# Mixing with features folded a second time, rows exchanged through DRAM, and the first chunk's norm moved

## The chip, the cores and the metric

One core of a Trainium2 chip runs the whole kernel. The metric is the device time of an execution in microseconds. Engines: PE is TensorE (matmuls; PEld its weight loads), DVE VectorE, ACT ScalarE, POOL GpSimd, SP the engine that issues the DMAs.

## The reference

Attention with a sigmoid in place of the softmax, for 8 batches, 12 heads, 448 tokens, 64 features a head; then a mixing layer by Fourier transforms over tokens and features, and a feed-forward net:

```
scores = q @ k.T / sqrt(64) - log(448);  attn = sigmoid(scores);  x = (attn @ v)   as [8, 448, 768]
u  = x + real(fft(fft(x, axis=1), axis=2))
un = (u - mean(u)) / sqrt(var(u) + 1e-6)          over the 768 features
y  = u + relu(un @ w_ch1) @ w_ch2                 768 -> 3072 -> 768
```

All inputs and outputs are float32.

## The kernel before

**Stages.** The 3584 rows (8 batches of 448) go through attention and mixing batch by batch, and `u` is stored to DRAM (`u_dram`). Then the feed-forward net runs on seven chunks of 512 rows: the first plainly (`up_proj`, `down_proj`), interleaved with the end of the mixing, the other six with a fast matrix product of seven partial products (`fast_up`, `fast_down`). In the attention stage the weights are also read, split and stored again (`weight`, 48 blocks), and brought into their final form (`pair`) from step 180 on.

**The steps of the attention stage.** The loop `for t in range(0, TQ + 12, 2)` is an order written out by hand. A batch has 24 steps, a group of four heads eight. In each pass PE gets scores, the functions that `at(t, ...)` has put into `extra` for two steps are called in the order in which they were put there, then the values (`values`) or, in every fourth pass, a part of the mixing (`mix_some`) follow. `pin` ties the instructions of each engine to this order, so every engine works strictly in it.

**The folds.** `values` leaves x transposed in `xT` [128 features, 6 blocks, 2 halves of tokens, 225]. Blocks p and p + 3 make a pair. `fold` makes six additions or subtractions a pair, 18 a batch, all on POOL: features d and d + 384 (level 0, `eo`), the two halves of the tokens (level 1, `fd`), tokens n and 224 − n (level 2, into `xp`). `FOLDS` names their steps: pair 0 at 12 to 17, pair 1 at 20 to 25, pair 2 at 28 and 29, when its block is there.

**The mixing.** From step 34 of a batch on its pieces stand in the list `units`, and the first part is run at step 36, the others at 44 and 52. `stage_d` transforms along the features: for each `kp`, `c` (cosine or sine) and parity `par` of the frequency, three matmuls with 193 columns of `cd_sb` add up the three pairs. ACT copies the result to `A`. `stage_s` transforms along the tokens with 385 columns; ACT copies one result to `Q`, DVE forms `sm` and `df`. `add_x` transposes x on PE, three blocks at a time, and DVE adds it: `u`. SP stores the rows. The last batch's mixing runs after the loop, between pieces of `up_proj`.

**The norm of the first chunk** (`norm`, two groups of 256 rows): load (n = 0), statistics (1), the reciprocal root in small DVE instructions on [128, 2] (`rsqrt`, 2 to 5), scaling on DVE (7), a float16 copy `hl` on ACT (8), the rest on DVE and two transposing DMAs on SP for each 128 rows (9). `hl` has one buffer. `norm_plan` gives the steps, `at(96 + 32 * g + n, fn)` their start.

**ACT's other work** in the stage: `sigmoid` after every score product, `cast`, the absolute value of the weights, `xT`. All DMAs are issued by SP.

Of the kernel before, what the change touches and what calls it, by code (L numbers as in the profile page):

```python
# [19 lines left out]
HM = 113  # L20
HS = 225
# [4 lines left out]
CP = 128  # L26
CH = 64
# [4 lines left out]
FOLDS = ((12, 13, 14, 15, 16, 17), (20, 21, 22, 23, 24, 25), (28, 28, 28, 29, 29, 29))  # L32
# [19 lines left out]
def spectral_attention_ffn(tc, qk, v, w1, w2, cd, cs, ident_in, out):  # L52
# [8 lines left out]
    with ExitStack() as top:  # L61
# [4 lines left out]
        w_dram = dram.tile([2, NP, 128, 2, 7, 384], F16, name="w_dram")  # L66
        ident = cpool.tile([128, 128], F32, name="ident")
# [13 lines left out]
        if True:  # L81
# [87 lines left out]
            def values(gg, w):  # L169
                b, r = divmod(gg, NG)  # L170
                p = r + 3 * w
                vr, ps = vrs[gg], avs[gg][w]
                for c in range(3):
                    a = att.pop((2 * gg + w, c))
                    for j in range(2):
                        h = c * 256 + (2 * w + j) * D
                        nc.tensor.matmul(  # L177
                            ps[j * D:(j + 1) * D, :SQ], vr[:, h:h + D], a[:, j], start=False, stop=(c == 2))
                if r == 0 and w == 0:
                    xp = wst[0].tile([128, 2, 8, 384], F16, tag="ws", name="xp", bufs=3)  # L180
                    xp = xp.rearrange("p x s n -> p (x s n)").bitcast(F32)[:, :24 * HM]
                    xts[b] = (fx.tile([128, 6, 2, HS], F32, tag="xT", name="xT", bufs=2),
                              xp.rearrange("p (f c r i s) -> p f c r i s", f=2, c=2, r=2, i=3))
# [3 lines left out]
            eos = {}  # L187

            def fold(b, p, n, e):

                xT, xp = xts[b]
                lv, n = divmod(n, 2)
                op = (ALU.add, ALU.subtract)[n]
                if lv == 0:
                    if n == 0:
                        eos[p] = [fx.tile([128, 2, 2, HS], F32, tag=t, name=t) for t in ("eo", "fd")]
                    e.tensor_tensor(out=eos[p][0][:, n], in0=xT[:, p], in1=xT[:, p + 3], op=op)  # L197
                elif lv == 1:
                    eo, fd = eos[p]
                    e.tensor_tensor(out=fd[:, n], in0=eo[:, :, 0], in1=eo[:, :, 1], op=op)  # L200
                else:
                    fd = eos[p][1]
                    e.tensor_tensor(
                        out=xp[:, n, :, :, p], in0=fd[:, :, :, 0:HM], in1=fd[:, :, :, HS - 1:HM - 2:-1], op=op)

            def mix_units(b):
                xT, xp = xts[b]
                A = fx.tile([HM, 2, 2, 386], F32, tag="A", name="A")
                ps_d, sd, ut = {}, {}, {}

                def stage_d(kp, c, par, p):
                    m = HM - kp
                    if par == 0 and p == 0:
                        ps_d[c, kp] = ps_m.tile([128, 512], F32, tag="m", name="psd")
                    ps = ps_d[c, kp]
                    nc.tensor.matmul(
                        ps[:HM, par * 193:par * 193 + 193], xp[:, kp ^ c, c, par, p],
                        cd_sb[:, c, par, p], start=(p == 0), stop=(p == 2))
                    if par == 1 and p == 2:
                        act_next.append(lambda: nc.scalar.activation(  # L220
                            A[:, kp, c].rearrange("s (i r) -> s r i", r=2),
                            ps[:HM, 0:386].rearrange("s (r i) -> s r i", r=2), AF.Copy))

                def stage_s(kp, c):
# [3 lines left out]
                        ps[:m, :385], cs_sb[:HM, kp, c, :m], A[:, kp, c, :385], start=True, stop=True)  # L228
                    if c == 1:
                        sd["Q", kp] = Q = fx.tile([128, 385], F32, tag="Q", name="Q", bufs=2)  # L230
                        act_next.append(lambda: nc.scalar.activation(Q[:m], ps[:m, :385], AF.Copy))
                    else:
                        Q = sd["Q", kp]
                        sd[kp] = [fx.tile([128, 385], F32, tag=n, name=n) for n in ("sm", "df")]
                        for o, op in zip(sd[kp], (ALU.add, ALU.subtract)):
                            dve_next.append(lambda o=o, op=op: nc.vector.tensor_tensor(
                                out=o[:m], in0=ps[:m, :385], in1=Q[:m], op=op))

                def add_x(kp, r, hf):
# [7 lines left out]
                    for i in range(3):  # L247
                        nc.tensor.transpose(
                            ps[:HM - kp, i * 128:(i + 1) * 128], xT[:, hf * 3 + i, r, kp:HS:2], ident)
                    y = d if hf == r else s  # L250
                    m = HM - kp
                    ysl = y[:m, 384:0:-1] if hf else y[:m, 0:384]

                    def add():
                        nc.vector.tensor_tensor(
                            out=u[:m, hf * 384:hf * 384 + 384], in0=ps[:m, :384], in1=ysl, op=ALU.add)
# [11 lines left out]
                def units_d(kp, c):  # L268
                    return [(0.33, lambda par=par, p=p: stage_d(kp, c, par, p)) for par in range(2) for p in range(3)]
# [59 lines left out]
            def weight_row():  # L329
# [4 lines left out]
                row = cpool.tile([128, 128], F32, name="row")  # L334
# [43 lines left out]
            def rsqrt(c, n):  # L378
                mv = mvs[c]
                a, r, t = (mv[:, n] for n in range(2, 5))  # L380
                if n == 2:
                    nc.vector.tensor_scalar(out=a, in0=mv[:, 1], scalar1=1e-6, scalar2=None, op0=ALU.add)

                    nc.vector.tensor_scalar(
                        out=t.bitcast(I32), in0=a.bitcast(I32), scalar1=1, scalar2=None,
                        op0=ALU.logical_shift_right)
                    nc.vector.tensor_scalar(
# [3 lines left out]
                nc.vector.tensor_tensor(out=t, in0=r, in1=r, op=ALU.mult)  # L391
                nc.vector.scalar_tensor_tensor(
                    out=t, in0=t, scalar=-0.5, in1=a, op0=ALU.mult, op1=ALU.mult)
                nc.vector.scalar_tensor_tensor(
# [8 lines left out]
            def norm(c, i, n, pool):  # L403
# [8 lines left out]
                elif n < 6:  # L412
                    rsqrt(c, n)
# [130 lines left out]
            at(22, lambda: (nc.sync.dma_start(cs_sb, cs), nc.sync.dma_start(ident, ident_in)))  # L544
# [8 lines left out]
            at(TP + 2, weight_row)  # L553
# [503 lines left out]
def _layout(q, k, v, w1, w2):  # L1057
    import numpy as np
    B = q.shape[0]

# [11 lines left out]
    cd = np.zeros((128, 2, 2, 3, 193), np.float32)  # L1072
    d = np.arange(384).reshape(3, 128)
    for par in range(2):
        l = np.arange(par, 385, 2)
        ang = (d[:, :, None] * l) % 768
        for c, fn in enumerate((np.cos, np.sin)):
# [3 lines left out]
            cd[:, c, par, :, :len(l)] = m.transpose(1, 0, 2)  # L1081
# [3 lines left out]
    for kp in range(2):  # L1085
        ang = (n[:, None] * np.arange(kp, HS, 2)) % S
        half = np.where(n % 112 == 0, 0.5, 1.0)[:, None]
        for c, fn in enumerate((np.cos, np.sin)):
# [4 lines left out]
            "id_in": np.eye(128, dtype=np.float32)}  # L1093
# [28 lines left out]
```

## Time and profile before

| | us |
|---|---|
| median of 3 runs (1579.94 to 1580.24) | 1580.02 |
| the profiled execution | 1579.31 |
| its span, first to last instruction | 1577.5 |
| PE busy | 1557.6 |
| DVE busy | 1277.3 |
| ACT busy | 656.1 |
| POOL busy | 323.3 |

The profile is one execution. Busy is the time in which an engine had at least one instruction at work; the ends of pipelined matmuls are modelled. The attention stage reaches to about 380 us of the span, the first chunk to 580.

### The profile page before, as it was taken

The page shows a single profiled execution, that of the slowest core. Times are in us where ns is not written, and L with a number is a line of the kernel's source. Part 1 is how long each engine was busy: PE and PEld are TensorE (multiplying, and loading weights), DVE is VectorE, ACT ScalarE, POOL GpSimd, SP SyncE. Part 2 cuts the span into 40 slices and gives each one's busy share as a digit, 9 for nine tenths or more (in the row PEclk, how much of TensorE's full clock was granted, in tenths as well). Part 3 has the DMA queues.
Part 4 walks back from the last instruction along what each step waited for, and adds up shares of the span by engine and source line. Part 5 has one row for each costly group of instructions (what it writes and reads, how often), then busy time and mean ns, then how long its engine had stood idle before and what let it go on. Part 6 is the DMA issues. An engine that isn't in the chain of part 4 may idle for free.

```text
span 1577.5 us, 27405 instructions
## 1 busy us (share of the span) xinstructions
PE 1557.6 (99%) x11059; PEld 1064.9 (68%) x11059; DVE 1277.3 (81%) x2352; ACT 656.1 (42%) x780; POOL 323.3 (20%) x244
## 2 busy tenths in 40 slices
PE   8999999999999999999999999999999999999998
PEld 3556565566555567777777777777777777777775
DVE  4987788794799956887888888888788878887778
ACT  8777777665555424322232233232423232323221
POOL 3644344355898810000000000000000000000000
PEclk9999999999999999999999999999999999999999
DMA  7887878793788877659667866866676777576571
GB/s 293 312 313 274 308 262 306 260 302 105 286 281 291 322 306 302 200 220 313 233 192 284 258 233 226 306 200 256 258 255 195 282 290 234 167 300 254 199 269 56
DMA packets 130399, 402.43 MB, mean 255 GB/s; under 512 B 68832, under 2 KB 70112, under 8 KB 111712
## 3 DMA queue, kind: packets, MB, share of 16 engines
q1 hardware_dynamic: 130272, 400.68, 71.1%
q8 instruction: 86, 1.41, 0.4%
q14 instruction: 41, 0.34, 0.1%
HBM read 311.39 MB, written 73.92 MB: 244 GB/s over the span
## 4 chain that ended last, share of the span: by engine, by line
PE 67%; DVE 5%; DMA 1%; issue 1%; ACT 1%; SPq 0%; DVEq 0%; ACTq 0%
PE psf L851 30%; PE pso L908 29%; PE po L627 4%; PE psh L607 3%; DVE wp L458 2%; DVE F L857 1%; DMA U<-u_dram 1%; DMA ws<-w_dram 1%; DVE ur L936 0%; DVE H L857 0%; ACT H L886 0%; DVE hl L615 0%; DVE ur L648 0%; DVE acc L1006 0%; DVE acc L923 0%
## 5 line engine op out<-in xcount | busy, mean ns | idle before, releaser
L851 PE MATMUL psf<-ut,ws 128*128 128x256 f16 x4536 | 506.8, 273 | 0.5 <-DMA ws<-w_dram 0.3
L908 PE MATMUL pso<-ws,H 128*128 128x384 f16 x3024 | 503.4, 326 | 1.0 <-DVE H L857 0.9
L851 PEld LDWEIGHTS <-ws 128*128 128x128 f16 x4536 | 443.6, 98 | 60.0 <-DMA ws<-w_dram 0.9
L908 PEld LDWEIGHTS <-H 128*128 128x128 f16 x3024 | 295.6, 98 | 189.9 <-DVE H L857 1.7
L876 ACT ACTIVATE F<-F 128x1024 f32<-128x1024 f32 x72 | 76.1, 1057 | 407.0 <-DVE F L857 407.0
L923 DVE TENSOR_TENSOR acc<-pso,acc 128x384 f32<-128x384 f32 x399 | 207.3, 548 | 19.7 <-PE pso L908 19.7
L857 DVE TENSOR_TENSOR H<-F,H 128x1024 f16<-128x1024 f32 (+1 forms) x144 | 155.2, 1086 | 48.9 <-ACT H L886 48.7
L886 ACT ACTIVATE H<-F 128x1792 f16<-128x1792 f32 x72 | 122.2, 1697 | 110.7 <-DVE F L857 110.7
L127 ACT ACTIVATE a<-sc 128x900 f32<-128x900 f32 x168 | 147.1, 921 | 48.3 <-PE sc L139 47.5
L857 DVE TENSOR_TENSOR F<-X,psf 128x256 f32<-128x256 f32 x288 | 116.8, 417 | 60.0 <-PE psf L851 55.5
L466 POOL TENSOR_TENSOR wq<-wq 128x384 f32<-128x384 f32 x96 | 153.4, 1605 | 29.7 <-DVE wp L458 24.1
L857 DVE TENSOR_TENSOR F<-F 128x256 f32<-128x256 f32 x288 | 109.4, 421 | 24.8 <-ACT F L876 20.2
L177 PE MATMUL av<-a,vr 128*64 128x450 f32 x576 | 119.1, 549 | 0.0
L458 DVE SCALAR_TENSOR_TENSOR wp<-wq,wsc,wp 128x1536 f16<-128x1536 f32 x48 | 99.1, 2096 | 16.8 <-ACT wp L456 16.8
L857 DVE TENSOR_TENSOR X<-X,psf 128x256 f32<-128x256 f32 x216 | 89.5, 414 | 16.9 <-PE psf L851 15.3
L607 PE MATMUL psh<-ut,wp 128*128 128x512 f16 x432 | 98.5, 379 | 0.0
L197 POOL TENSOR_TENSOR eo<-xT 128x450 f32<-128x450 f32 x48 | 52.0, 1104 | 209.8 <-ACT xT L185 209.8
L865 ACT ACTIVATE X<-psf 128x256 f32<-128x256 f32 x72 | 27.8, 386 | 154.0 <-PE psf L851 154.0
L627 PE MATMUL po<-wp,hh 128*128 128x256 f16 (+1 forms) x384 | 88.5, 326 | 0.0
L177 PEld LDWEIGHTS av<-a,vr 128*64 128x64 f32 x576 | 37.1, 136 | 69.2 <-issue 69.2
L456 ACT ACTIVATE wp<-wq,wsc 128x1536 f16<-128x1536 f32 x48 | 73.6, 1570 | 23.4 <-DMA wq<-t_dram 17.9
L607 PEld LDWEIGHTS <-wp 128*128 128x128 f16 x432 | 42.3, 98 | 49.4 <-issue 0.7
(93 smaller groups left out, 1604.5 us busy)
## 6 DMA issues: line engine op xcount, KB each, us to landing
ws<-w_dram SPq DMA_DIRECT2D x144, 1344.0 KB, 7.3
wr<-w_in SPq DMA_DIRECT2D x48, 768.0 KB, 6.0
w_dram<-wp SPq DMA_DIRECT2D x24, 1344.0 KB, 8.0
qk<-qk_in SPq DMA_DIRECT2D x23, 898.0 KB, 6.7
t_dram<-wt SPq DMA_DIRECT2D x48, 384.0 KB, 5.8
wq<-t_dram SPq DMA_DIRECT2D x24, 768.0 KB, 5.3
vr<-v_in SPq DMA_DIRECT2D x24, 448.0 KB, 4.1
U<-u_dram SPq DMA_DIRECT2D x24, 384.0 KB, 9.2
```

The lines of the kernel that those rows point to most:

```text
L127: nc.scalar.activation(a, ps[:, :, :SQ], AF.Sigmoid, bias=-math.log(S), scale=1.0 / math.sqrt(D))
L177: nc.tensor.matmul(ps[j * D:(j + 1) * D, :SQ], vr[:, h:h + D], a[:, j], start=False, stop=(c == 2))
L458: nc.vector.scalar_tensor_tensor(out=w[:, 1, part], in0=t, scalar=sc, in1=w[:, 0, part], op0=ALU.mult, op1=ALU.subtract)
L466: nc.gpsimd.tensor_tensor(out=t[:, o], in0=t[:, x], in1=t[:, y], op=op)
L607: nc.tensor.matmul(hs[c, f], l[:, m], r[:, m], start=(m == n == 0), stop=(m == NCC - 1 and n == 2))
L627: nc.tensor.matmul(po[n][:, at:at + hi - lo], l[:, cols], r[:, lo:hi], start=(f == 0 and m == 0 and at == 0), stop=(f == NFC - 1 and m == ...
L851: nc.tensor.matmul(ps[:, :TH], w[:, x, a, m * 128:(m + 1) * 128], ut[y][:, b, m], start=(m == n == 0), stop=(m == n == 2))
L857: nc.vector.tensor_tensor(out=o, in0=x, in1=y, op=op)
L876: nc.scalar.activation(F[:, 0:4], F[:, 0:4], AF.Relu)
L886: nc.scalar.activation(hts[P][:, 0], F[:, 1:8], AF.Copy)
L908: nc.tensor.matmul(ps[:, :384], H[:, x, a, tp * 128:(tp + 1) * 128], w[:, y, b], start=(j == n == 0 and half != 1), stop=(j == 1 and n == ...
L923: later(0, lambda: nc.vector.tensor_tensor(out=to, in0=ps[:, :384], in1=to, op=ALU.add))
```

## The change

- **Features folded again.** In level 2 the pair 1 is added to and subtracted from pair 2 (features d against 384 − d), so that two blocks of 128 remain where three were. `stage_d` adds two matmuls for three, with 198 columns for 193; `A`, `Q`, `sm`, `df` have 396 columns. The columns of the result, of the weights and of the output stand in another order, which the host takes back; `add_x` transposes against permutations (`perm`) instead of the identity. The heads are put in another order and some of `v` is reversed by the host, so that features that belong together lie in one partition.
- **Hops.** Three rows lie in a wrong partition. `turn_rows` carries them to a DRAM tile at step 25 and back into other partitions at step 30, with two DMAs each time, issued by ACT.
- **The order of the folds.** Pairs 0 and 1 make four additions each (steps 12 to 15, 20 and 21), pair 2 four at step 28, and six follow at step 31: two between the pairs, four into `xp`. In the last batch DVE does the odd ones from step 28 on.
- **The norm.** The groups start 48 steps apart (32 before), the copies `hl` at 23 and 35 (19 and 27), the rest and the transposes at 25 and 37 (22 and 30). The iterations of `rsqrt` run on POOL, in four instructions where DVE had three.
- Weight blocks that ended at steps 154 and 162 end at 130 and 170; `weight_row` comes two steps later and borrows a tile.

```diff
+HEADS = [0, 5, 4, 3, 1, 2, 6, 11, 10, 9, 7, 8]
-FOLDS = ((12, 13, 14, 15, 16, 17), (20, 21, 22, 23, 24, 25), (28, 28, 28, 29, 29, 29))
+FOLDS = ((12, 0, 0), (13, 0, 1), (14, 0, 2), (15, 0, 3), (20, 1, 0), (20, 1, 1), (21, 1, 2), (21, 1, 3),
+         (28, 2, 0), (28, 2, 1), (28, 2, 2), (28, 2, 3), (31, 2, 5), (31, 2, 4), (31, 0, 7), (31, 2, 7), (31, 0, 6), (31, 2, 6))
+NB = 66
+NL = 6 * NB
+        turn = dram.tile([2, 3, 4, HS], F32, name="turn")
-            cd_sb = c1.tile([128, 2, 2, 3, 193], F32, name="cd_sb")
+            cd_sb = c1.tile([128, 2, 2, 2, NL // 2], F32, name="cd_sb")
+            perm = c1.tile([128, 3, 128], F32, name="perm")
...
             def fold(b, p, n, e):
-                xT, xp = xts[b]
+                xT, xp, last = xts[b]
+                if p == 0 and n == 0:
+                    fds[b] = fx.tile([128, 2, 4, HS], F32, tag="fd", name="fd")
+                fd = last if p == 2 else fds[b][:, p]
...
+                elif lv == 2:
+                    k = slice(1, 3) if n else slice(0, 4, 3)
+                    e.tensor_tensor(out=fd[:, k], in0=fd[:, k], in1=fds[b][:, 1, k], op=op)
                 else:
-                    fd = eos[p][1]
+                    fd = fd.rearrange("p (c r) n -> p c r n", c=2)
                     e.tensor_tensor(
-                        out=xp[:, n, :, :, p], in0=fd[:, :, :, 0:HM], in1=fd[:, :, :, HS - 1:HM - 2:-1], op=op)
+                        out=xp[:, n, :, :, 1 - p // 2], in0=fd[:, :, :, 0:HM], in1=fd[:, :, :, HS - 1:HM - 2:-1], op=op)
+
+            def turn_rows(b, back):
+                fd, tmp = fds[b], turn[b % 2]
+                pairs = ((fd[64:65], tmp[1:3] if back else tmp[0:2]), (fd[0:1, 1:2], tmp[0:1] if back else tmp[2:3]))
+                for x, y in pairs:
+                    x, y = x.rearrange("o a k n -> o (a k n)"), y.rearrange("(o a) k n -> o (a k n)", o=1)
+                    nc.scalar.dma_start(*((x, y) if back else (y, x)))
...
-                        ps[:HM, par * 193:par * 193 + 193], xp[:, kp ^ c, c, par, p],
-                        cd_sb[:, c, par, p], start=(p == 0), stop=(p == 2))
+                        ps[:HM, par * NL // 2:(par + 1) * NL // 2], xp[:, kp ^ c, c, par, p],
+                        cd_sb[:, c, par, p], start=(p == 0), stop=(p == 1))
...
-                        ps[:m, :385], cs_sb[:HM, kp, c, :m], A[:, kp, c, :385], start=True, stop=True)
+                        ps[:m, :NL], cs_sb[:HM, kp, c, :m], A[:, kp, c], start=True, stop=True)
...
-                            ps[:HM - kp, i * 128:(i + 1) * 128], xT[:, hf * 3 + i, r, kp:HS:2], ident)
+                            ps[:HM - kp, i * 128:(i + 1) * 128], xT[:, j, r, kp:HS:2], perm[:, n])
...
-            def rsqrt(c, n):
+            def rsqrt(c, n, e=nc.vector):
...
+                e.tensor_tensor(out=t, in0=r, in1=r, op=ALU.mult)
+                if e is nc.gpsimd:
+                    e.tensor_tensor(out=t, in0=t, in1=a, op=ALU.mult)
+                    e.tensor_scalar(out=t, in0=t, scalar1=-0.5, scalar2=1.5, op0=ALU.mult, op1=ALU.add)
+                    e.tensor_tensor(out=r, in0=t, in1=r, op=ALU.mult)
+                    return
...
-                    rsqrt(c, n)
+                    rsqrt(c, n, nc.vector if n == 2 else nc.gpsimd)
...
-                    for n, t in ((1, 10), (7, 17), (8, 19 + 8 * j), (9, 22 + 8 * j)):
+                    for n, t in ((1, 10), (7, 17), (8, 23 + 12 * j), (9, 25 + 12 * j)):
...
-                for r, when in enumerate(FOLDS):
-                    for n, t in enumerate(when):
-                        at(24 * b + t, lambda b=b, r=r, n=n: fold(b, r, n, nc.gpsimd))
+                for t, p, n in FOLDS:
+                    e = nc.vector if b == B - 1 and t > 27 and n % 2 else nc.gpsimd
+                    at(24 * b + t, lambda b=b, p=p, n=n, e=e: fold(b, p, n, e))
+                for k, t in enumerate((25, 30)):
+                    at(24 * b + t, lambda b=b, k=k: turn_rows(b, k))
...
-                          + [(t, (-10, -2, -1, 0, 3)) for t in (34, 58, 82, 154, 162, 178)])
+                          + [(t, (-10, -2, -1, 0, 3)) for t in (34, 58, 82, 130, 170, 178)])
...
-            at(TP + 2, weight_row)
+            at(TP + 4, weight_row)
...
-                        at(96 + 32 * g + n, fn)
+                        at(96 + 48 * g + n, fn)
```

## Rows read from the trace of the kernel before

**Rows 1.** The page, part 1: busy time, share of the span and instructions of an engine.

```profile
PE 1557.6 (99%) x11059; PEld 1064.9 (68%) x11059; DVE 1277.3 (81%) x2352; ACT 656.1 (42%) x780; POOL 323.3 (20%) x244
```

**Rows 2.** Busy time by stretch. The stretches are cut at the first matmul of a batch's mixing: batches 1, 2, 3, 5 and 6 (counted from 0). Columns: the stretch, its length, busy time of PE, PEld, DVE, ACT and POOL with their instructions, granted clock, share of the DMA engines, GB/s.

```profile
57.92:105.34 47.42, 46.84 (x311) 27.72 (x309) 44.04 (x59) 35.24 (x48) 23.82 (x19) 1.00 0.82 290
105.34:152.43 47.09, 46.60 (x311) 27.77 (x309) 37.61 (x54) 34.91 (x47) 19.45 (x19) 1.00 0.82 295
152.43:199.51 47.08, 46.59 (x310) 27.76 (x308) 37.57 (x55) 34.16 (x46) 19.43 (x19) 1.00 0.85 319
247.38:299.31 51.93, 49.19 (x311) 28.87 (x309) 42.80 (x71) 34.62 (x46) 17.80 (x18) 0.97 0.73 256
299.31:348.06 48.75, 47.09 (x311) 28.25 (x309) 42.87 (x60) 36.03 (x49) 22.48 (x19) 1.00 0.95 316
```

**Rows 3.** The chain of work that ended last, in order of time, between 403 and 470 us (start, length, what), and PE's timeline where this part ends.

```profile
403.05 0.34 DVE wp L458
...
419.09 9.83 DMA U<-u_dram
...
457.47 1.93 DVE U L399 x2
...
460.75 0.66 PE L731 MATMUL pst<-ident,U 128*128 128x128 f32 x4 [1.00 <-DVE hl L615]
```

**Rows 4.** Groups of instructions by line and shape: the two transforms' matmuls on PE. After the bar: busy time, mean ns of one, idle time before them.

```profile
L216 PE MATMUL psd<-cd_sb,xp 128*113 128x193 f32 x384 | 68.8, 329 | 0.0
L227 PE MATMUL pss<-A,cs_sb 113*112 113x385 f32 x32 | 13.6, 506 | 0.0
L227 PE MATMUL pss<-A,cs_sb 113*113 113x385 f32 x32 | 13.1, 489 | 1.2 <-ACT A L220 1.2
```

**Rows 5.** PE in order of time, the start of the mixing of batch 2 (start, length of the run, what).

```profile
152.43 4.19 PE L216 MATMUL psd<-cd_sb,xp 128*113 128x193 f32 x24
156.45 0.81 PE L227 MATMUL pss<-A,cs_sb 113*113 113x385 f32 x2
157.10 0.49 PE L216 MATMUL psd<-cd_sb,xp 128*113 128x193 f32 x2
```

**Rows 6.** ACT and PE in order of time in batch 5 and at the beginning of batch 6's stretch, and busy time by stretch (columns as in rows 2) for the matmuls behind the longest wait.

```profile
281.67 0.84 ACT L422 ACTIVATE hl<-un 128x768 f16<-128x768 f32 x1 [2.79 <-DVE un L399]
...
300.49 0.84 ACT L422 ACTIVATE hl<-un 128x768 f16<-128x768 f32 x1 [2.94 <-DMA ut<-hl]
...
285.84 0.87 PE L248 MATMUL psx<-ident,xT 128*112 128x128 f32 x3 [1.93 <-ACT Q L231]
...
304.68 0.90 PE L227 MATMUL pss<-A,cs_sb 113*113 113x385 f32 x2 [1.19 <-ACT A L220]
...
287.73:289.91 2.18, 2.18 (x14) 1.69 (x13) 2.18 (x4) 0.58 (x1) 1.38 (x2) 0.61 0.16 65
```

**Rows 7.** Groups of instructions by line and shape: POOL's folds, the small operations of the root on DVE, and a memset on POOL.

```profile
L203 POOL TENSOR_TENSOR xp<-fd 128x452 f32<-128x452 f32 x48 | 62.5, 1324 | 1.9
L200 POOL TENSOR_TENSOR fd<-eo 128x450 f32<-128x450 f32 x48 | 55.2, 1170 | 1.9
L197 POOL TENSOR_TENSOR eo<-xT 128x450 f32<-128x450 f32 x48 | 52.0, 1104 | 209.8 <-ACT xT L185 209.8
L391 DVE TENSOR_TENSOR mv<-mv 128x2 f32<-128x2 f32 x42 | 11.0, 261 | 0.3
L392 DVE SCALAR_TENSOR_TENSOR mv<-mv 128x2 f32<-128x2 f32 x42 | 9.8, 233 | 1.4
L1109 POOL MEMSET const-bfloat16-1.0<- 128x1 bf16 x1 | 0.1, 102 | 0.0
```

**Rows 8.** ACT in order of time around step 30 of batch 2, and the first and last rows of the six folds of a third pair on POOL, in batch 2 and in batch 0.

```profile
142.60 1.73 ACT L127 ACTIVATE a<-sc 128x900 f32<-128x900 f32 x2 [2.62 <-PE sc L139]
144.22 0.95 ACT L115 ACTIVATE hi<-qk 128x898 fp32r<-128x898 f32 x1
...
136.78 1.92 POOL L197 TENSOR_TENSOR eo<-xT 128x450 f32<-128x450 f32 x2 [9.51 <-ACT xT L185]
...
140.77 2.10 POOL L203 TENSOR_TENSOR xp<-fd 128x452 f32<-128x452 f32 x2
...
45.37 2.24 POOL L197 TENSOR_TENSOR eo<-xT 128x450 f32<-128x450 f32 x2 [2.57 <-ACT xT L185]
...
51.00 2.84 POOL L203 TENSOR_TENSOR xp<-fd 128x452 f32<-128x452 f32 x2
```

**Rows 9.** DMAs: the issue of the row stores on SP's queue (duration ns min/median/max) and their time from issue to landing; last the landing of the output stores of the later stage (L1014).

```profile
L263 SPq DMA_DIRECT2D u_dram<-u x48: 272/422/937, 81.2 to 410.0; - x48
DMA to landing us min/median/max: 2.9/5.1/8.9
...
DMA to landing us min/median/max: 2.3/2.3/3.0
```

**Rows 10.** The last batch, in order of time: the folds of its third pair on POOL, ACT's copy before them in its order, DVE's sum, and PE's first matmuls of the mixing.

```profile
377.62 1.92 POOL L197 TENSOR_TENSOR eo<-xT 128x450 f32<-128x450 f32 x2 [5.73 <-ACT xT L185]
...
381.62 2.08 POOL L203 TENSOR_TENSOR xp<-fd 128x452 f32<-128x452 f32 x2
...
377.82 0.49 ACT L231 ACTIVATE Q<-pss 112x385 f32<-112x385 f32 x1 [0.28 <-PE pss L227]
...
378.86 0.56 DVE L236 TENSOR_TENSOR sm<-pss,Q 112x385 f32<-112x385 f32 x1
...
384.25 2.13 PE L216 MATMUL psd<-cd_sb,xp 128*113 128x193 f32 x12
```

More of the change, by code (lines that the diff above doesn't have):

```diff
@@ L246, in add_x @@
                     ps = ps_m.tile([128, 512], F32, tag="m", name="psx")
[L247 removed]
+                    for i, (j, n) in enumerate((((0, 0), (1, 0), (2, 0)), ((3, 1), (5, 2), (4, 2)))[hf]):
                         nc.tensor.transpose(
[L249 to L250 removed]
+                            ps[:HM - kp, i * 128:(i + 1) * 128], xT[:, j, r, kp:HS:2], perm[:, n])
                     m = HM - kp
[L252 removed]
+                    y = (d if hf == r else s)[:m].rearrange("s (r b k) -> s b r k", r=2, k=NB)
+                    y = y[..., 0:64] if hf else y[..., 2:66]
                     def add():
[L255 to L256 removed]
+                        o, x = (t.rearrange("s (b r k) -> s b r k", r=2, k=64)
+                                for t in (u[:m, hf * 384:hf * 384 + 384], ps[:m, :384]))
+                        nc.vector.tensor_tensor(out=o, in0=x, in1=y, op=ALU.add)
                         if hf:
@@ L268, in units_d @@
                 def units_d(kp, c):
-                    return [(0.33, lambda par=par, p=p: stage_d(kp, c, par, p)) for par in range(2) for p in range(3)]
+                    return [(0.33, lambda par=par, p=p: stage_d(kp, c, par, p)) for par in range(2) for p in range(2)]
                 def units_s(kp, c):
@@ L333, in weight_row @@
                 top = cpool.tile([128, 1], F32, name="top")
-                row = cpool.tile([128, 128], F32, name="row")
+                row = fx.tile([128, DM], F32, tag="w5", name="wt")[:, :128]
                 nc.vector.tensor_reduce(out=top[:2], in_=ps[:2, :128], op=ALU.max, axis=AX.X)
@@ L1059, in _layout @@
     B = q.shape[0]
+    q, k, v = (a[:, HEADS] for a in (q, k, v))
+    v = v.copy()
+    for h in (2, 3, 8, 9):
+        v[:, h] = v[:, h][..., -np.arange(D) % D]
+    w1, w2 = w1[_columns()], w2[:, _columns()]
     qt, kt = (a.reshape(B, 2, NG, 2, S, D).transpose(0, 2, 1, 3, 5, 4).reshape(B, 2 * NG, 2 * D, S) for a in (q, k))
@@ L1071, in _layout @@
     w2t = np.ascontiguousarray(w2.reshape(NFC, 128, DM).transpose(1, 0, 2)).reshape(128, -1).view(np.int64)
-    cd = np.zeros((128, 2, 2, 3, 193), np.float32)
-    d = np.arange(384).reshape(3, 128)
+    cd = np.zeros((128, 2, 2, 2, NL // 2), np.float32)
+    r = np.arange(64)
+    d = np.stack([np.arange(64, 192), np.concatenate([r, [192], 321 + r[:63]])], axis=1)
+    h, places = _heads(), _places()
+    order = [np.concatenate([a for b, m in enumerate((1, 2, 2)) for a in (
+        384 - h[-b % 3][places[m, k, :2]], h[b][places[0, k]])]) for k in range(2)]
     for par in range(2):
-        l = np.arange(par, 385, 2)
+        l = order[par]
         ang = (d[:, :, None] * l) % 768
@@ L1092, in _layout, with _heads, _places, _columns @@
     return {"qk_in": qk, "v_in": vt, "w1_in": w1t, "w2_in": w2t, "cd_in": cd, "cs_in": cs,
-            "id_in": np.eye(128, dtype=np.float32)}
+            "id_in": np.stack([np.eye(128, dtype=np.float32)] + [
+                np.eye(128, dtype=np.float32)[:, p.ravel()] for p in _places()], axis=1)}
+def _heads():
+    import numpy as np
+    r = np.arange(64)
+    p = np.arange(128)
+    return np.stack([np.concatenate([r, 320 + r]), np.where(p % 64, 320 - p, 256 - p), 64 + p])
+def _places():
+    import numpy as np
+    res = np.zeros((3, 2, 64), int)
+    for k in range(2):
+        core = np.array([n for n in range(2, 128) if n % 64 > 1 and n % 2 == k])
+        ends = np.array([k, 64 + k])
+        res[0, k] = np.concatenate([core, ends])
+        res[1, k] = np.concatenate([(128 - ends) % 128 if k else ends, 128 - core])
+        res[2, k] = np.concatenate([ends, core])
+    return res
+def _columns():
+    import numpy as np
+    l, p = _heads(), _places()
+    half = [l[b][p[0].ravel()] for b in range(3)]
+    return np.concatenate(half + [384 + l[b][p[n].ravel()] for b, n in ((0, 1), (2, 2), (1, 2))])
 def _tokens():
```

50 lines of the change are left out of this document (25 added, 25 removed).

## Prediction, made before the change was run

> **What bounds the kernel now.** First the busy times of the page: TensorE (PE) 99% of the span, VectorE (DVE) 81%, GpSimd (POOL) 20% [rows 1]. An average can hide a stage, so next the busy times batch by batch, cut at the first matmul of each mixing: batches take 47.1 us, and in an undisturbed one PE is idle for 0.5 us only, DVE for 9.5, ScalarE (ACT) for 12 [rows 2]. In the attention stage PE therefore sets the pace, with two exceptions: the stretch of 51.93 us, where PE is idle for 2.7 us and its granted clock falls, and the 48.75 us after it. Last the chain of waits: from 403 to 461 us it runs over the weight pairs on DVE and a load, though PE is idle there for only 1.0 us; after it PE is the chain [rows 3]. So a microsecond of PE work taken out of a batch is a microsecond gained as long as nothing PE waits for comes later than the new PE order wants it.
>
> **The feature matmuls.** `stage_d` issues 4·2·3 = 24 matmuls in a batch, 16 after. A float32 matmul shows as two instructions: 8·24·2 = 384 [rows 4]. In a back-to-back run 24 of them take 156.45 − 152.43 = 4.02 us, 0.168 each [rows 5] (the 329 ns of the group is latency, overlapped). Removed: 128 · 0.168 = 21.5 us. The remaining 256 have 198 columns for 193: 256 · 0.168 · 5/193 = 1.1 us back. The 64 instructions of `stage_s` have 396 for 385 columns at (157.10 − 156.45)/2 = 0.325 us: 64 · 0.325 · 11/385 = 0.6 us back. Net −19.8 us. The transposes (L248) keep their number and width; only their moving operand is another tile. The weight loads go down with the matmuls.
>
> **The evictions** read 396 for 385 or 386 columns, 3% of 0.56 us each for the sums on DVE [rows 10]; the permuted write of `A` becomes a plain one. DVE and ACT have room for that: nothing.
>
> **The norm of the first chunk.** In batch 5 ACT waits at 281.67 us for the scaling of rows on DVE (2.79 us) before the copy `hl`, and at 300.49 for the transposing DMA that still reads the only `hl` (2.94 us). Behind these copies in ACT's order stand the copies `Q` and `A`, and PE waits for them: 1.93 and 1.19 us [rows 6]. After the first wait the granted clock is 0.61 between 287.73 and 289.91, so most of that stretch ran at 1.2 GHz instead of 2.4 [rows 6]. The price of it all is 51.93 − 47.08 = 4.85 us, and 1.19 in the next batch: 6.0 us. After the change the copy comes six steps after the scaling (two before), and the second ten steps after the first's transposes are issued (five before); a step is 47.1/24 = 1.96 us, so both waits should be covered. Moved with it are one 768 KB load, the statistics, the scaling, `hl` twice and the transposes of the second group, past SP's weight loads and into steps 144 to 181; two weight blocks move to ends at 130 and 170. In that place SP has the weight stores and `wq` loads behind the transposes, due some steps later. What they meet there no row shows: between the whole 6.0 us gained and none. I take 4.5, since the two named causes go and the stretch as a whole remains busy (DVE 42.87 of 48.75 us).
>
> The root goes to POOL in 12 tiny instructions a group. A 128x2 operation takes 0.23 to 0.26 us on DVE; on POOL it lies between a memset's 0.10 and a fold's 1.10 [rows 7]. Nearest in size is DVE's: 12 · 0.26 = 3.1 us (1.2 to 13.2) against the six steps, 11.8 us, before DVE scales with it. Behind it on POOL are the folds of pair 0, due 13 steps later. Nothing taken; the top end costs 1.4 us twice.
>
> **The folds and the hops.** POOL's count stays at 18 additions a batch. What matters is the time by which the last lie ready. Before, the six of the third pair start when its `xT` is there, and need nothing else. Now six wait for rows that two DMAs of ACT carry to DRAM at step 25 and two more carry back at step 30, and the first mixing matmul stands at step 36. The first hop has five steps, 9.8 us, to land. The second is tight. In batch 2 ACT is through with the sigmoids of step 30 at 144.22, where its issues now stand; PE comes to the matmuls at 152.43 [rows 5, 8]. The gap is 8.2 us. The first four matmuls (8 · 0.168 = 1.34 us) need four of the six additions, the others all six; so 9.55 us for: two issues of 0.35 (SP's for the row stores: 0.27 to 0.94 [rows 9]), the landing L, and six POOL additions. These take 6.1 us when POOL is undisturbed (136.78 to 142.87), 8.5 in batch 0 (45.37 to 53.84) [rows 8], and by the means of the three lines 2·(1.10+1.17+1.32) = 7.2 us [rows 7]. The stall is 0.7 + L + 7.2 − 9.55 = L − 1.65 us a batch. No row shows a DMA as small as 7.2 KB on an own queue. The landings shown: 2.3 us for the output stores of the later stage, 2.9 the least and 5.1 the median of the row stores of this one [rows 9]. I take 2.3, since a small transfer alone on its queue has nothing ahead of it: 0.65 us in each of seven batches, 4.5 us. Bounds: an L of 1.65 or less, or a clean POOL (2.3 + 0.7 + 6.1 = 9.1), gives nothing; L = 5.1 gives 3.45 · 7 = 24 us.
>
> The notes agree with the low end: the Trainium skill, DMA: Bandwidth & Descriptors, section Anatomy of one DMA, puts the fixed cost of a DMA at about 2.0 us (for GpSimd's own path), most of it the write receipt; with 2.0 the stall would be, as an estimate, 0.35 · 7 = 2.5 us. Against the change speaks GPSIMD Engine Reference of the Trainium skill, section Key points: GpSimd shares its SBUF interfaces with VectorE and contends with operations of two SBUF inputs. The spread between 6.1 and 8.5 us agrees with it. If it held in every batch, the stall would be 2.3 + 0.7 + 8.5 − 9.55 = 1.95 us, 13.7 in all.
>
> ACT pays four issues a batch, 1.4 us, of the 12 it has idle [rows 2]. They stand between sigmoids, which free the banks of the scores: 0 to 2 us in all, 0.5 taken. If ACT's hop waited for late folds, everything behind it would: the folds of step 20 have 9.8 us for some 5, so no.
>
> **The last batch.** Its `xT` is there at 377.6 us, POOL ends its folds at 383.7, PE wants them at 384.25 [rows 10]. Now DVE, idle for most of that time, does half. The back hop is issued behind `Q` at 378.3: + 0.7 + 2.3 = 381.3, then an addition on each engine (1.1), and DVE's two (0.55 each) for the first matmuls at 383.5, POOL's two at 384.6, needed 1.34 later. It fits, but DVE waits for POOL ahead of work that PE needs (`sm`, `df`): 0 to 4 us, 1.5 taken. The mixing there is 8 · 0.336 = 2.7 us shorter; if the chain over DVE from 403 to 461 does not start earlier with it, up to 2.7 us is lost; this is part of the 4.
>
> DVE has 44.04 of 47.42 us in batch 1 [rows 2]; in 44.9 us it would be busy 98%. 0.5 taken, 0 to 2.
>
> **The sum**, against the profiled execution: −19.8 − 4.5 + 4.5 + 0.5 + 1.5 + 0.5 = −17.3 us. That execution took 1579.3 us (span 1577.5, 1.8 around it), 0.7 under the median of the runs. 1580.0 − 17.3 = 1562.7.
>
> **Rivals.**
> - The hop is hidden: POOL clean, or L below 2. No stall, no trouble at the end: −19.8 − 6.0 + 0.5 = −25.3, 1554.7 us. For it: the undisturbed set of 6.1 us; against: batch 0.
> - The gain is taken by another engine: DVE at 98% in batch 1, DMA at 0.95 in the 48.75 us stretch, the chain from 403 us. With the norm's waits back in another place (nothing of the 4.5), and the top ends 2 + 4 + 2 of the last three terms: −19.8 + 4.5 + 8 = −7.3, 1572.7 us.
> - Slower: the hop lands as late as SP's own stores. At L = 5.1 the stall is 24 us: −19.8 − 4.5 + 24 + 2.5 = +2, 1582 us, no change; from about 5.2 on the kernel is slower by more than a measurement's error, and at 8.9 [rows 9] the stall is 51 us, 1609. For it: the DMA engines are busy 82 to 95% of these stretches [rows 2], and all of the row stores landed in 2.9 or more. Against: those were large or queued behind large ones of the same queue. What would help it: the skill's page on DMA, section Queues, rings and completion order, has each DMA engine take turns between the queues by packets; by that the small hop passes the large loads and this rival falls away.
>
> **Chances.** Forecast 0.40, its own range 1558 to 1568; hidden 0.30, 1552 to 1558; another engine 0.17, 1568 to 1577; the late hop 0.13, from 1577 on. The range leaves out most of the last and some of each end: 1553 to 1575. No change is within 0.2%, 3.2 us, about what a measurement of this kernel can tell. Faster: 0.40 + 0.30 + 0.17 and a little of the late hop's lower end, 0.89; same 0.05; slower 0.06.
>
> **What would show it.** L216: 256 instructions, some 46 us busy. The batches: 44.5 us and the stall; PE idle before the first L216 of a batch, released by POOL, is the hop. The landing of the DMAs on ACT's queue gives L. The 51.93 us stretch and ACT's waits before `hl` should be gone; if a wait of some us for `hl`, for the small POOL instructions, or for the folds in front of the sigmoids stands elsewhere, the norm's term or the hop's is wrong. From 610 us on all should be as before, only earlier.

## The result, and the profile after

The changed kernel takes 1593.97 us (1591.99 to 1595.35) beside 1580.13 us for the kernel before on the same chip: ratio 1.0084, interval 1.0072 to 1.0096. It is slower by 0.84%, 13.3 us by the ratio (13.8 between the two medians), where 17.3 us less was forecast, and above the upper end of the range. The spans of the two profiled executions are 1577.5 and 1590.2 us. The first feature matmul of the last batch's mixing stands at 384.25 us before [rows 10] and at 396.58 after: 12.3 of the 12.7 us are lost by then, in the attention stage.

The stretches of the changed kernel, cut as in [rows 2] at the first matmul of a batch's mixing, all seven:

```profile
59.35:106.01 46.66, 45.72 (x292) 26.66 (x293) 38.17 (x50) 33.47 (x46) 21.46 (x19) 0.97 0.73 250
106.01:154.81 48.80, 46.14 (x292) 26.37 (x292) 40.94 (x54) 34.66 (x46) 23.30 (x19) 0.97 0.81 284
154.81:205.96 51.15, 46.35 (x293) 25.70 (x293) 44.84 (x62) 34.37 (x47) 22.23 (x19) 0.97 0.83 304
205.96:253.79 47.83, 44.49 (x292) 25.19 (x293) 42.04 (x56) 37.05 (x50) 24.85 (x31) 1.00 0.80 278
253.79:304.36 50.57, 47.69 (x293) 27.08 (x293) 43.41 (x59) 32.77 (x45) 21.46 (x19) 0.93 0.85 293
304.36:357.51 53.15, 45.90 (x293) 26.07 (x293) 47.90 (x62) 37.31 (x50) 25.93 (x31) 0.97 0.76 261
357.51:396.58 39.07, 34.76 (x206) 19.99 (x206) 21.70 (x36) 17.07 (x23) 17.59 (x15) 1.00 0.49 139
```

Of the first six only one has PE's expected work of about 44.5 us, the one with a granted clock of 1.00; and in each of the seven PE is idle for 1 to 7 us, where it was 0.5 in an undisturbed stretch before [rows 2]. The cause is in the waits. PE's waits up to 396.58 us (total, times, longest):

```profile
PE psd L237 <- POOL xp L216: 15.8, 12, 2.3
PE psx L268 <- DVE u L277: 5.2, 2, 4.4
PE sc L145 <- ACT a L133: 5.1, 7, 1.7
PE psd L237 <- DVE xp L216: 1.2, 1, 1.2
```

The same view of the kernel before has no wait of these kinds but the third, with 1.8 us, and two behind ACT's copies (`Q` 1.9, `A` 1.2 us) that are gone now. The balance up to the last batch:

| | us |
|---|---|
| feature matmuls, 7/8 of the net 19.8 | −17.3 |
| PE idle: 13.2 before (384.25 − 371.07 busy), 34.4 after (396.58 − 362.13) | +21.3 |
| PE busy 371.07 → 362.13, that is 8.9 less and not 17.3 | +8.4 |
| sum | +12.4 |

The last row but one is put down to the clock: behind the waits the same matmuls take longer. The kernel without the hop (below) agrees: with the same matmuls and few waits, PE is busy for 355.25 us up to the last batch's mixing, where 371.07 − 17.3 = 353.8 was due. The mixing of batch 1 shows it all. In order of time: ACT's two issues of the back hop, POOL's six additions, DVE beside them, and PE.

```profile
96.39 0.20 ACTq L225 DMA_DIRECT2D fd<-turn  x1
96.62 0.27 ACTq L225 DMA_DIRECT2D fd<-turn  x1
...
99.64 2.98 POOL L213 TENSOR_TENSOR xp<-xp,fd 128x450 f32<-128x450 f32 x2 [5.83 <-DMA fd<-turn]
102.57 1.92 POOL L216 TENSOR_TENSOR xp<-fd 128x452 f32<-128x452 f32 x1
...
107.77 1.66 POOL L216 TENSOR_TENSOR xp<-xp 128x452 f32<-128x452 f32 x1
...
98.68 0.96 DVE L338 SCALAR_TENSOR_TENSOR wt<-wr,wt 128x768 int32<-128x768 int32 x1
99.67 1.94 DVE L340 SCALAR_TENSOR_TENSOR wt<-wr,wt 128x768 int32<-128x768 int32 x1
...
106.01 1.60 PE L237 MATMUL psd<-cd_sb,xp 128*113 128x198 f32 x8 [0.45 <-POOL xp L216]
109.48 2.32 PE L237 MATMUL psd<-cd_sb,xp 128*113 128x198 f32 x8 [1.87 <-POOL xp L216]
```

And the busy times of the stretch behind the second wait, columns as above:

```profile
109.48:111.80 2.32, 2.32 (x9) 2.23 (x10) 2.29 (x2) 0.00 (x0) 2.24 (x3) 0.66 1.06 368
```

The hop lands 2.75 us after its issue (96.89 to 99.64). Then the six additions take 9.8 us, to 109.43, where a clean set of six took 6.1 [rows 8]; a DVE operation that runs at 0.96 us takes 1.94 beside them. PE waits twice, and the second eight matmuls take 2.32 us for 1.60, at a granted clock of 0.66: after the wait most of the stretch ran at 1.2 GHz.

### The profile page after: what moved, and what is told of

Same layout as the page of the kernel before. It is cut to its first block, busy times and chain, and to the rows that moved or that the text cites. A ratio compares the mean times of both kernels' runs of the same rounds, so it can differ in the third digit from the quotient of the medians.

```text
span 1590.2 us, 27197 instructions
## 1 busy us (share of the span) xinstructions
PE 1546.8 (97%) x10931; PEld 1048.5 (66%) x10931; DVE 1288.0 (81%) x2339; ACT 655.5 (41%) x780; POOL 328.7 (21%) x263
## 4 chain that ended last, share of the span: by engine, by line
PE 66%; DVE 5%; DMA 2%; ACT 1%; issue 1%; POOL 0%; SPq 0%; DVEq 0%; ACTq 0%; POOLq 0%
PE psf L880 29%; PE pso L937 29%; PE po L656 4%; PE psh L636 3%; DVE wp L484 1%; DMA ws<-w_dram 1%; DMA U<-u_dram 1%; DVE F L886 1%; DVE ur L965 0%; DVE H L886 0%; ACT H L915 0%; DMA wq<-t_dram 0%; DVE ur L677 0%; POOL wq L492 0%; DVE acc L1035 0%
## 5 line engine op out<-in xcount | busy, mean ns | idle before, releaser
L492 POOL TENSOR_TENSOR wq<-wq 128x384 f32<-128x384 f32 x96 | 150.1, 1569 | 32.3 <-DVE wp L484 23.5
L207 POOL TENSOR_TENSOR eo<-xT 128x450 f32<-128x450 f32 x47 | 55.3, 1196 | 156.2 <-ACT xT L192 156.2
```

The source lines that it names most:

```text
L492: nc.gpsimd.tensor_tensor(out=t[:, o], in0=t[:, x], in1=t[:, y], op=op)
```

## The experiments

**The hop left out.** The calls of `turn_rows` are removed, so the rows that it exchanges stay on their old partitions; all else is the changed kernel.

```
-                for k, t in enumerate((25, 30)):
-                    at(24 * b + t, lambda b=b, k=k: turn_rows(b, k))
```

> The changed kernel without the two hops of a batch (three rows of the folded features keep a wrong partition). Theory A, the last six additions are late because they wait for the second hop and then run slowly: PE's waits for POOL before the first feature matmuls (15.8 us) and before the last batch (1.2) go, and with them most of the 8 us that the lower granted clock costs behind such waits: 1594 - 24 = 1570 us. Theory B, the moved norm and weight blocks cost the time (ACT's late sigmoids in batches 3 and 5, DVE's late sums in batch 6): less than 6 us are gained, 1588 or more.

1570.49 us (1568.90 to 1570.87), ratio to the kernel before 0.9929 (0.9915 to 0.9944). PE's waits for POOL fall to 0.6 us, the clock is 0.997. So the late last additions, with what hangs on them, cost 23 us; the norm's new place does not explain the loss. What remains is the backlog on DVE: a wait of 4.5 us for `u`.

**The hop earlier.** All of the work, with ACT's issues at steps 23 and 26.

```
-                for k, t in enumerate((25, 30)):
+                for k, t in enumerate((23, 26)):
```

> The changed kernel with the hops at steps 23 and 26 in place of 25 and 30; everything is computed. Theory A: the rows are back before pair 2 is folded, so the six additions start behind POOL's own four and end some 5 us earlier; the time is within 4 us of the kernel without hops, about 1570. Theory B: within 6 us of 1594.

1571.87 us (1569.91 to 1574.16), ratio 0.9938 (0.9922 to 0.9955): faster than both kernels. POOL's wait for the DMA is gone and PE's waits for POOL are 0.8 us. The additions are as slow as ever, and now PE hardly waits for them. Its stretches, third to sixth:

```profile
151.68:197.17 45.49, 44.42 (x294) 25.39 (x292) 40.65 (x54) 33.71 (x46) 22.19 (x18) 1.00 0.93 343
197.17:241.84 44.67, 44.18 (x295) 25.38 (x293) 43.29 (x62) 34.92 (x47) 30.80 (x30) 1.00 0.79 267
241.84:288.54 46.70, 44.68 (x295) 25.31 (x293) 41.05 (x54) 34.65 (x48) 22.70 (x18) 1.00 0.99 346
288.54:339.69 51.15, 46.63 (x295) 26.96 (x293) 50.08 (x71) 35.98 (x49) 31.36 (x31) 0.93 0.77 264
```

44.18 us of PE work against 46.59 before [rows 2] is 2.4 us a batch, the 19.8/8 of the forecast. In the last of these lines DVE has become the bound: 50.08 of 51.15 us. Where PE does not wait, the first 16 feature matmuls of a batch run in one piece:

```profile
151.68 2.94 PE L237 MATMUL psd<-cd_sb,xp 128*113 128x198 f32 x16
```

**The norm part, in two kernels.** First the changed kernel with the norm's steps, its root and the two weight blocks as in the kernel before:

```
-                    rsqrt(c, n, nc.vector if n == 2 else nc.gpsimd)
+                    rsqrt(c, n)
...
-                    for n, t in ((1, 10), (7, 17), (8, 23 + 12 * j), (9, 25 + 12 * j)):
+                    for n, t in ((1, 10), (7, 17), (8, 19 + 8 * j), (9, 22 + 8 * j)):
...
-                          + [(t, (-10, -2, -1, 0, 3)) for t in (34, 58, 82, 130, 170, 178)])
+                          + [(t, (-10, -2, -1, 0, 3)) for t in (34, 58, 82, 154, 162, 178)])
...
-                        at(96 + 48 * g + n, fn)
+                        at(96 + 32 * g + n, fn)
```

> The changed kernel with the first chunk's norm, its root on DVE and the weight blocks at the steps of the kernel before; folds and hops as changed. Theory A: the waits for POOL stay, the two new waits in batches 3, 5 and 6 (some 9 us with their clock) go and the old ones for the copy hl (6 us) come back: 1589 to 1595. Theory B: about 1580 or less.

1593.63 us (1592.19 to 1595.68), ratio 1.0079: the same as the changed kernel, as Theory A had it. PE's wait for `u` is down to 0.8 us, and ACT's waits for the copies `hl` are back (4.8 and 3.4 us). Then the reverse, the kernel before with the same lines changed as in the diff (48 steps, root on POOL, blocks 130 and 170) and nothing else:

> The kernel before with the norm's part of the change alone (groups 48 steps apart, later copies, iterations of the root on GpSimd, weight blocks at 130 and 170). My prediction's term: 4.5 us faster, 1575.5; the bounds were 1574 and 1580. Theory B: slower than before by 5 us or more.

1582.14 us beside 1580.98, ratio 1.0010 (1.0000 to 1.0019): neither expectation. ACT's waits of [rows 6] for `hl` are gone, and another wait of PE has come, 5.79 us at 336.38; PE of that kernel:

```profile
336.38 2.18 PE L248 MATMUL psx<-ident,xT 128*112 128x128 f32 x9 [5.79 <-DVE u L255]
```

It is the same place as in the changed kernel, where DVE in order of time has this ahead of `u` (idle nowhere):

```profile
335.43 0.95 DVE L452 TENSOR_TENSOR hl<-un,hl 128x768 f16<-128x768 f32 x1
336.30 1.34 DVE L335 TENSOR_SCALAR wt<-wt 128x768 int32<-128x768 int32 x1
337.67 1.62 DVE L338 SCALAR_TENSOR_TENSOR wt<-wr,wt 128x768 int32<-128x768 int32 x1
339.32 1.62 DVE L340 SCALAR_TENSOR_TENSOR wt<-wr,wt 128x768 int32<-128x768 int32 x1
340.87 0.55 DVE L277 TENSOR_TENSOR u<-psx,df 113x384 f32<-113x384 f32 x1
...
341.47 1.85 PE L268 MATMUL psx<-perm,xT 128*112 128x128 f32 x9 [4.35 <-DVE u L277]
```

**Early hop with the old norm.** Both edits, steps 23 and 26 and the norm lines above.

> Changed kernel with its hops at steps 23 and 26, and with the norm, its root on VectorE and the weight blocks where the kernel before has them; nothing of the computation is left out. If the moved norm is worth nothing here either, as in the kernel before with this part alone: 1571 to 1573 us, as the early hop with the moved norm. If the predicted 4.5 us were only hidden behind the late hop: 1576, with ACT's waits for the copies hl and a lowered clock in batch 5. If the moved norm costs (VectorE in front of step 172): 1567 to 1568.

1586.76 us (1582.55 to 1592.45), ratio 1.0043 (1.0027 to 1.0059): none of the three expectations. Beside the early hop alone the norm's new place is worth some 15 us (14.9 between the medians, which come from two chips). Its stretches that answer to the last three of the early hop above, and under them ACT's waits for the copy `hl` from 190 to 360 us (total, times, longest):

```profile
195.25:246.58 51.33, 46.60 (x295) 26.11 (x293) 43.06 (x69) 35.36 (x48) 22.17 (x19) 0.97 0.80 257
246.58:298.65 52.07, 48.49 (x295) 26.69 (x293) 47.65 (x74) 34.26 (x46) 20.45 (x18) 0.93 0.71 251
298.65:351.28 52.63, 47.20 (x294) 26.71 (x292) 42.05 (x58) 36.04 (x49) 22.84 (x19) 0.94 0.87 299
```

```profile
ACT hl L448 <- DVE un L425: 7.9, 2, 5.1
ACT hl L448 <- DMA ut<-hl: 4.1, 1, 4.1
```

They are 13.5 us longer in all. In the kernel before, the same two rows of this view read 5.4 us (two waits, one of them the 2.79 of [rows 6]) and 2.9. PE's waits for ACT's copies `A`, `Q` and `xT`, which follow in ACT's order, are 12.0 us here and 1.5 with the early hop alone (3.5, 3.3, 2.9 and 2.3 us against 0.9 and 0.6). Why the waits for `hl` have grown is open. A step is shorter in time in an undisturbed batch (44.7 us a batch for 47.1), so the same distance in steps covers less; that was not tested, and the three stretches above are longer than that.

**Two DVE operations fewer.** The changed kernel, hops at 25 and 30, without the two operations of each weight block that read two SBUF operands; the weights are then not the reference's.

```
-                    nc.vector.scalar_tensor_tensor(
-                        out=ti, in0=lo, scalar=29, in1=ti, op0=ALU.logical_shift_right, op1=ALU.bitwise_or)
-                    nc.vector.scalar_tensor_tensor(
-                        out=ti, in0=hi, scalar=-0x40000000, in1=ti, op0=ALU.bitwise_and, op1=ALU.bitwise_or)
```

> Changed kernel, hops at steps 25 and 30, with the two VectorE operations of each weight block that read two SBUF operands (scalar_tensor_tensor on 128x768) left out, so that the weights are not the reference's. Theory A1 (the additions on GpSimd are slow because these two operations share their access to SBUF): the six additions take about 6.1 to 6.5 us in all mixings that now take 8.9 to 9.8, the landing stays at 2.7 to 2.8 us, and PE's idle time released by GpSimd falls from 15.8 us to 2 to 5; the time is about 1575. Theory A2 (the landing and ACT's order are the delay, and the additions are slow for another reason): the additions still take 9 us, PE's wait stays above 12 us, the time stays above 1585 but for what VectorE saves.

1577.66 us in one run, PE's waits for POOL 11.6 us. POOL and PE at the mixing of batch 1:

```profile
103.98 2.56 POOL L213 TENSOR_TENSOR xp<-xp,fd 128x450 f32<-128x450 f32 x2 [8.01 <-DMA fd<-turn]
106.49 1.06 POOL L216 TENSOR_TENSOR xp<-fd 128x452 f32<-128x452 f32 x1
...
109.79 1.06 POOL L216 TENSOR_TENSOR xp<-xp 128x452 f32<-128x452 f32 x1
...
108.74 1.60 PE L237 MATMUL psd<-cd_sb,xp 128*113 128x198 f32 x8 [1.04 <-POOL xp L216]
```

The six additions take 6.9 us (103.98 to 110.85), and 6.7 to 7.5 in the seven batches, where 6.1 to 6.5 were expected: most of their slowness comes from these DVE operations. But the landing, expected at 2.75, is 4.9 us (issued by 99.10), so more of the wait stays than the 2 to 5 us expected. The landing varies for another reason. These are stretches from the end of the back hop's second issue to POOL's first addition, first four of the changed kernel, then two of this one:

```profile
96.89:99.64 2.75, 2.75 (x22) 0.92 (x16) 2.68 (x5) 2.75 (x4) 0.00 (x0) 1.00 0.61 248
145.85:147.81 1.96, 1.96 (x18) 0.64 (x12) 1.89 (x5) 1.96 (x3) 0.00 (x0) 1.00 0.53 216
242.90:247.69 4.79, 4.79 (x38) 2.04 (x32) 4.69 (x8) 4.73 (x7) 0.00 (x0) 1.00 0.98 351
347.07:351.29 4.22, 4.22 (x32) 1.82 (x24) 4.15 (x6) 4.18 (x6) 0.00 (x0) 1.00 1.01 403
```

```profile
99.10:103.98 4.88, 4.88 (x38) 2.15 (x32) 4.81 (x9) 4.81 (x7) 0.00 (x1) 1.00 1.02 414
145.65:150.73 5.08, 5.08 (x38) 2.18 (x32) 4.97 (x11) 5.05 (x8) 0.00 (x1) 1.00 1.01 403
```

The length is the landing, the last column but one the share of the DMA engines. Of the fourteen such stretches in the two kernels the twelve with a share of 0.93 or more took 3.71 to 5.08 us, the two with 0.53 and 0.61 took 1.96 and 2.75. So a long landing goes with full DMA engines. That they are its cause was not tested, and of the seven stretches of the changed kernel with the old norm one does not fit: 4.18 us at a share of 0.27.

```profile
146.01:150.19 4.18, 4.18 (x32) 1.75 (x26) 4.08 (x7) 4.18 (x6) 0.00 (x1) 1.00 0.27 112
```

The other six do: 1.44 to 2.48 us at 0.03 to 0.86, 4.12 to 5.37 at 1.01 or more.

**The hop on SP.** One word, hops at 25 and 30.

```
-                    nc.scalar.dma_start(*((x, y) if back else (y, x)))
+                    nc.sync.dma_start(*((x, y) if back else (y, x)))
```

> Changed kernel, hops at steps 25 and 30, but issued by SP instead of ACT, so that they stand in the queue of the loads and row stores; nothing of the computation is left out. Theory A (L as short as 2.75 us because the queue is its own): on SP's queue the hop lands with the row stores, 4 to 9 us, PE waits some 40 us for the last additions, 1605 to 1625 us. Rival (ACT's blocked issues of 2 us in batches 3 and 5 cost more than the queue helps): ACT's waits and PE's waits for the sigmoids go, the landing stays near 3 us, and the time is 1588 to 1591.

1590.89 us in one run, so the expected 1605 to 1625 was wrong. The rival's time was met, but not by its landing near 3 us: in the seven batches the landing is 5.9 to 8.3 us. In batch 1 SP, free of the sigmoids, issues at 94.80 to 95.37, and POOL starts at 102.61: 7.2 us. PE comes to the matmuls at 109.29, so the issue is 14.5 us ahead of it where ACT's was 9.2 (96.39 to 105.56): SP's queue lands the hop 4.5 us later after its issue, nearly all of the 5.3 us by which it is issued earlier. PE's waits for POOL are 17.3 us; its waits for the sigmoids fall from 5.1 to 1.4 us, so those did come from ACT's issues. In the changed kernel ACT is through with the pair in batch 3 only after 2.03 us, four times that of batch 1. Each of the two issues takes 0.20 us there too; the second begins at 196.0, 1.8 us after the first. ACT does nothing from 193.51 to 196.29, and the profile puts the end of that idle time down to the landing of the norm's load:

```profile
194.21 2.03 ACTq L225 DMA_DIRECT2D fd<-turn  x2
196.29 0.95 ACT L121 ACTIVATE hi<-qk 128x898 fp32r<-128x898 f32 x1 [2.79 <-DMA un<-u_dram]
...
198.89 0.71 PE L145 MATMUL sc<-hi 64*128 64x450 f32 x2 [1.71 <-ACT a L133]
```

**DVE's weight block moved.** Three kernels with the early hop, in which the block that ends at step 170 ends at 162, 106 or 146; the second as an example:

```
-                          + [(t, (-10, -2, -1, 0, 3)) for t in (34, 58, 82, 130, 170, 178)])
+                          + [(t, (-10, -2, -1, 0, 3)) for t in (34, 58, 82, 106, 130, 178)])
```

> Changed kernel with its hops at steps 23 and 26 and with one weight block ending at step 162 instead of 170, so that VectorE has no weight block in front of the mixing of step 172; nothing of the computation is left out. Theory A (the six last additions come too late: the hop's landing plus slow additions on GpSimd; the rest of the loss is VectorE's order around step 172): PE's wait of 4.4 us for u in batch 6 is gone, batch 6 falls from 51.2 us to about 47, and the whole is 4 us faster than the early hop alone: about 1567 to 1568 us. Theory B (DVE is full in these batches wherever the block lies): the wait moves into batch 5 and the time stays at 1571 to 1573.

> Changed kernel with hops at steps 23 and 26, and the weight block that ends at step 170 moved to one that ends at 106; nothing of the computation is left out. Theory C (with the hop out of the way VectorE is the bound of batch 5, from step 156 to 180, where it is busy 46.8 to 50.1 us because its weight blocks, the second group's norm and GpSimd's additions meet): PE's waits for u (2.9 and 0.8 us) and the lowered clock behind them go, that batch falls from 50.1 us to about 46, the batch of steps 84 to 108 rises by at most 1 us, and the time is about 1567 to 1568 us. Rival (VectorE's work only moves: 4 us more between steps 84 and 108, where it is busy 40.7 of 45.4 us, give the wait there): 1571 to 1573.

> The same with the block at step 146 instead of 106, in the batch of steps 132 to 156, where VectorE is busy 41.3 of 46.6 us and the DMA engines' share is highest; nothing of the computation is left out. Theory C: VectorE would be busy some 45.5 us there, more than TensorE's 44.7, so about 1 us is lost there of the 4 gained: 1568 to 1569. Rival: the wait moves with the block, 1571 to 1573.

1572.23, 1572.29 and 1571.90 us, ratios 0.9946, 0.9945 and 0.9946: no difference from the early hop alone, as the rivals had it in all three. ("Batch 5" in the expectation for 106 is the stretch that begins with the mixing of batch 5, 291.04 to 335.76 us below.) With the block at 106 the two stretches in question are:

```profile
196.42:244.78 48.36, 45.66 (x294) 25.41 (x293) 47.00 (x66) 34.48 (x47) 31.13 (x30) 1.00 0.87 294
...
291.04:335.76 44.72, 44.20 (x295) 25.34 (x293) 42.58 (x60) 35.06 (x48) 31.19 (x31) 1.00 0.80 275
```

The place emptied is at PE's pace, 44.72 for 51.15 us; the place filled has lost 3.7 us (48.36 for 44.67). And what is left is lost behind the last batch: its mixing starts at 376.65 us with the early hop, 375.49 with 162 and 374.62 with 106, but DVE scales `U` of the next norm (457.47 us before [rows 3]) at 450.68, 450.60 and 450.46. The chain of waits there runs over the weight pairs on DVE and the load of `U` (11.40 us at 411.26 with 106, 6.88 at 411.63 with the early hop alone).

## Why the prediction was wrong

**The feature matmuls** were right: 256 instructions at (2.94 − 1.60)/8 = 0.168 us each, from the undisturbed runs of 16 and of 8 above, and 2.4 us less PE work a batch.

**The hop's stall** was the step that failed, by its two sizes. The sum was issues + L + six additions − 9.55, with 0.7, 2.3 and 7.2: 0.65 us a batch. In the seven batches the issues took 0.5 (2.0 to 2.1 in two, 1.02 in one), L was 1.96 to 4.8, median 4.3, and the additions took 7.3 to 10.4, mean 8.8. The form of the sum holds: in batch 1, 0.5 + 2.75 + 9.8 against a gap that was 10.5 (from 96.39 to 105.56, where PE comes, and 1.34) makes 2.5, and PE waited 0.45 + 1.87. In all 15.8 us for 4.5, within the bound of 24. Two choices did it. L was taken from output stores of a later stage instead of the row stores of this one (2.9 to 8.9 [rows 9]); alone on its queue the hop still took 3.7 to 5.1 us in the stretches with a DMA share of 0.93 or more. This case's landings speak against the inference that I drew from the Trainium skill's page DMA: Bandwidth & Descriptors, section Queues, rings and completion order, that taking turns between queues would let a small hop pass; on SP's queue it did land later still, at 5.9 to 8.3 us, so an own queue helps in part. And the additions were taken at means over folds that mostly ran elsewhere in the batch; at their new place they lie beside weight blocks. The sentence from the Trainium skill's GPSIMD Engine Reference, section Key points, that told against the change described this; the run without the two-operand operations agrees (6.9 us for 9.8), and DVE's own 0.96 became 1.62 to 1.94. The price stood in the trace of the kernel before: the set of 8.5 us in batch 0 [rows 8] ran beside a weight block, the set of 6.1 us in batch 2 beside none. DVE in batch 0:

```profile
46.80 1.62 DVE L317 SCALAR_TENSOR_TENSOR wt<-wr,wt 128x768 int32<-128x768 int32 x1
48.46 1.62 DVE L319 SCALAR_TENSOR_TENSOR wt<-wr,wt 128x768 int32<-128x768 int32 x1
```

The prediction had the 8.5 as a bound that gives 13.7 us in all; it was nearer to the measured 8.8 and 15.8 us than the 7.2 that was taken.

**The clock** had no term. A clock of 0.61 behind a wait was there to see [rows 6]; the prediction used it for the old stall and gave new stalls only their idle time. By the balance it cost 8.4 us beside 21.3 us of added idle time, and it went away with the waits: without the hop the mean clock of the span is 0.997, with it 0.993.

**The norm** was taken at −4.5. The two named waits went, and a wait that takes the place of the one removed came: the moved weight block and the second group's `hl` stand ahead of `u` on DVE (4.35 us after, 5.79 with the norm part alone). In the kernel before and in the changed one the part is worth nothing (+1.2 and +0.3 us, neither clear of nothing). Its value is not one number: with the early hop it is some 15 us. The DVE term, 0.5 for batch 1 alone, looked at the wrong batch.

**ACT's issues** were costed at 0.5 with 2 as the bound; PE's waits for the sigmoids grew by 3.3 us, over the bound, nearly all of it (1.71 and 1.64) behind the two pairs of issues that took 2.0 and 2.1 us. **The root on POOL** cost nothing there, as taken: its operations take 0.19 to 0.20 us alone. **The last batch**: PE waits 1.23 us for DVE's half of the folds and 1.80 for `A`; from the first feature matmul of that batch to the end it is 1193.6 us for 1193.25, so the 2.5 us of matmuls saved there were lost again: 2.9 us for the 1.5 taken, within its 4.

**The rivals.** The slower one had the mechanism, landings of 4 to 5 us beside full DMA engines, but put the point at L = 5.2 with additions of 7.2 us. Slower additions, the clock and the missing 4.5 us brought it to L = 4.3. Of the rival in which another engine takes the gain, two conditions came true beside it: the norm's waits are back in another place here, and the chain over DVE behind the last batch holds the time with the early hop.

**What stays open.** The early hop stays 9 us above the forecast. DVE is busy 39 to 50 us of its stretches of 45 to 51; moving one block moved the wait, and a second limit stands behind the last batch. Which single order would give both back was not found. Why the landings differ as they do, and why the second of ACT's issues begins 1.8 to 1.9 us after the first in two batches, was not separated: in the changed kernel the profile names the landing of the norm's 768 KB load at both places, but with the old norm one of the two stayed (2.07 us for the pair), and there it names an operation of DVE.

## What to carry to other kernels

When work is put behind a small DMA on the path of the engine that sets the pace, give the landing the time that DMAs of this stage take while the DMA engines are full, and each addition the time it has beside its new neighbours on the other engine; issues two and four steps earlier were worth 22 us here. A new wait of PE costs its idle time and then the slower matmuls behind it. A move that is worth nothing alone can be worth much with a saving, as the norm's was here (nothing, and some 15 us), and has to be tried with it; that the shorter steps are the reason was not shown.

## What the hardware showed that was not expected

- A hop of 7 and 3.5 KB on ACT's queue landed in 2.0 to 2.75 us with the DMA engines at 0.53 to 0.61 of their time and in 3.7 to 5.1 us at 0.93 or more (fourteen cases; of seven in another kernel one, 4.18 us at 0.27, does not fit).
- The contention of POOL's additions with DVE goes both ways: 0.98 to 1.07 us became 1.4 to 1.9 on POOL, and 0.96 became 1.62 to 1.94 on DVE; the operation with one SBUF input at L335 took 1.34 for 0.56. Beside DVE's batch statistics POOL's additions stayed at 1.07. The Trainium skill, SBUF — State Buffer, section Who interferes with whom, names both kinds of DVE operation (two SBUF inputs, and the fast mode that `tensor_scalar` can enter); the trace agrees.
- The issues of the back hop on ACT's queue took 0.20 to 0.29 us each, but in two batches the pair took 2.0 to 2.1 us, with 1.6 to 1.7 us between its two issues in which ACT does nothing.
